# Attention projections of a fused attention and two-MoE kernel: three split products against a diagonal weight become one fp32 product per head on its own 64 rows

## Chip, core and metric

One NeuronCore of a Trainium2 chip runs the whole program. The metric is the device time of one execution in microseconds. The kernel before takes 2019.83 us, the median of three runs (2019.09 to 2023.27).

## What is computed

The reference chains three layers; the change touches the first lines of the first one.

```python
def phi(x):                                   # x: q or k, (4, 8, 576, 64)
    proj = np.einsum('bhsd,df->bhsf', x, w_phi)          # w_phi: (64, 128)
    proj = proj - np.max(np.abs(proj), axis=-1, keepdims=True)
    return np.concatenate([np.exp(proj), np.exp(-proj)], axis=-1)
q_p, k_p = (phi(q), phi(k))
kv = np.einsum('bhsf,bhsd->bhfd', k_p, v)
z = np.sum(k_p, axis=2)
num = np.einsum('bhsf,bhfd->bhsd', q_p, kv)
den = np.einsum('bhsf,bhf->bhs', q_p, z)[..., None] + 1e-06
return (num / den).astype(np.float32)
```

The result, 2304 tokens of 512 features, goes through a mixture of experts with Sinkhorn routing (8 experts, all of them applied to all tokens) and through one with a single expert per token. These two layers take most of the time.

## The kernel before

**Units and steps.** The attention stage works on eight units: a pair of batches (`bp`) times a pair of heads (`h_`). The transposed inputs hold the two heads of a pair on partitions 0 to 63 and 64 to 127, and 1152 tokens (two batches) in the free dimension, cut into nine chunks of 128 tokens. `CH` groups them into five groups per unit: four of two chunks and one of a single chunk.

**One step.** `step` is called once per group. In program order it issues `qtr` (transposes of the previous group's q projection to feature-major, L183), `proj` for one k group and for one q group of the unit before (L144), `kvm` (the k side's product with v, summed over a unit in the banks B and C, L166), `xtr` (transposes of a finished group of results, L226) and `num` (numerator and denominator of one group, L195). At a *turn*, where a unit's last k group is summed, `kvm` comes first, then `qtr`, the q projection, the k projection, `xtr` and `num`. Seven turns have a k projection in them, one per boundary between two units; the first of these has no finished result for `xtr` yet. Each engine works its instructions off in this order; the five functions write one queue per engine.

**The projection.** The weight is a 128 x 256 tile with `w_phi` twice on its diagonal, so that one product over 128 rows gives both heads. To reach fp32 accuracy with the faster fp32r format, weight and input are split into a rounded part and a rest (`wbh`, `wbl`; `hi`, `lo`), and each chunk takes three products (L151 to L153) summed in one PSUM bank. `split_in` makes the input's parts: a cast on ScalarE (L122) and a subtract on GpSimd, or on VectorE for the first unit (L123). VectorE then takes the largest magnitude per token and head straight from PSUM (L155) and subtracts it (L157), both heads at once. For k, ScalarE applies the two exponentials (L161); for q they come after the transposes (L192).

**PSUM.** Eight banks: four buffers "A" (`proj`, `xtr`), one "B" and one "C" (`kvm`), two "D" (`qtr`, `num`). When only the last unit's q groups are left (`live["tail"]`), `proj` uses C and `xtr` uses B, because the first MoE's products take A. The pool gives a new tile one of its tag's buffers, and the new tile's first writer waits for the last reader of the old one.

**After num.** `num` ends on VectorE: add, reciprocal and multiply (L219, L220, L223) read its bank and write `xn`. `xtr` transposes `xn`, ScalarE copies it to `xo` (L234) and SP writes it out.

Of the kernel before, what the change touches and what calls it, by code (L numbers as in the profile page):

```python
# [11 lines left out]
F32 = mybir.dt.float32  # L12
F32R = mybir.dt.float32r
# [3 lines left out]
ALU = mybir.AluOpType  # L17
AX = mybir.AxisListType
# [3 lines left out]
B, H, S, D = 4, 8, 576, 64  # L22
# [3 lines left out]
P = 128  # L26
# [18 lines left out]
def build(tc, a, out):  # L45
# [5 lines left out]
    live = {}  # L51
# [8 lines left out]
    V, A, G, T, SP = nc.vector, nc.scalar, nc.gpsimd, nc.tensor, nc.sync  # L60
# [3 lines left out]
    def psum(tag, shape):  # L64
        n_ps[0] += 1
        bufs = {"A": 4, "B": 1, "C": 1, "D": 2}[tag]
        return live["pp"].tile(shape, F32, tag="ps" + tag, bufs=bufs, name=f"ps{tag}{n_ps[0]}")

    def f32(ap):
        return ap.bitcast(F32)  # L70
# [25 lines left out]
    ap_ = at.enter_context(tc.tile_pool(name="at", bufs=2))  # L96
    units = [(bp, hp_) for bp in (1, 0) for hp_ in range(KD)]
    NU = len(units)
    CH = [(0, 1), (2, 3), (4, 5), (6, 7), (8,)]
# [3 lines left out]
    def load_in(u, which, g):  # L103
        bp, h_ = units[u]
        cs = slice(CH[g][0] * P, (CH[g][-1] + 1) * P)
        r = ap_.tile([P, 2 * P], F32, tag="r" + which, bufs=3, name=f"r{which}{u}{g}")
        SP.dma_start(out=r[:, 0:cs.stop - cs.start], in_=a[which + "T"][bp, h_, :, cs])
        live["r" + which, u, g] = r

    def load_v(u):  # L110
        bp, h_ = units[u]
        v = ap_.tile([P, 2, 11 * W], F32, tag="v", name=f"v{u}")
        SP.dma_start(out=v, in_=a["v"][bp, h_])
        live["v", u] = v

    def split_in(u, which, g):
        r = live.pop(("r" + which, u, g))
        n = len(CH[g]) * P
        bufs = 3 if which == "k" else 2
        hi = ap_.tile([P, 2 * P], F32R, tag="h" + which, bufs=bufs, name=f"h{which}{u}{g}")  # L120
        lo = ap_.tile([P, 2 * P], F32R, tag="l" + which, bufs=bufs, name=f"l{which}{u}{g}")
        A.copy(hi[:, :n], r[:, :n])  # L122
        (V if u == 0 else G).tensor_tensor(out=lo[:, :n], in0=r[:, :n], in1=f32(hi[:, :n]), op=ALU.subtract)  # L123
        live["s" + which, u, g] = (hi, lo)

    def warm(n):
        ps = psum("D", [P, P])
        for _ in range(n):
            T.matmul(ps, ident, ident, start=True, stop=True)

    wphi = ap_.tile([P, 2 * P], F32, bufs=1, name="wphi")
    V.memset(wphi, 0.0)
    for g in range(2):
        SP.dma_start(out=wphi[g * D:(g + 1) * D, g * P:(g + 1) * P], in_=a["w_phi"])
    for g in range(3):
        load_in(0, "k", g)
    load_v(0)
    warm(10)
    wbh = ap_.tile([P, 2 * P], F32R, bufs=1, name="wbh")
    wbl = ap_.tile([P, 2 * P], F32R, bufs=1, name="wbl")  # L140
    V.tensor_copy(wbh, wphi)
    V.tensor_tensor(out=wbl, in0=wphi, in1=f32(wbh), op=ALU.subtract)

    def proj(u, which, g):  # L144
        hi, lo = live.pop(("s" + which, u, g))
        n = len(CH[g])
        ps = psum("C" if live.get("tail") else "A", [P, 2 * n, P])
        for c in range(n):
            o = ps[:, 2 * c:2 * c + 2, :].rearrange("p h f -> p (h f)")
            cs = slice(c * P, (c + 1) * P)  # L150
            T.matmul(o, hi[:, cs], wbh, start=True, stop=False)  # L151
            T.matmul(o, hi[:, cs], wbl, start=False, stop=False)
            T.matmul(o, lo[:, cs], wbh, start=False, stop=True)  # L153
        m = ap_.tile([P, 4], F32, tag="m", bufs=4, name=f"m{which}{u}{g}")[:, 0:2 * n]
        V.tensor_reduce(out=m, in_=ps, axis=AX.X, op=ALU.max, apply_absolute_value=True)  # L155
        pr = ap_.tile([P, 4, P], F32, tag="pr" + which, name=f"pr{which}{u}{g}")[:, 0:2 * n]
        V.tensor_tensor(out=pr, in0=ps, in1=m.unsqueeze(2).to_broadcast([P, 2 * n, P]), op=ALU.subtract)  # L157
        if which == "k":
            ek = ap_.tile([P, 4, 2, P], F32, tag="eq" if u == 0 and g == 2 else "ek", bufs=2, name=f"ek{u}{g}")
            for sg in range(2):  # L160
                A.activation(out=ek[:, 0:2 * n, sg, :], in_=pr, func=AF.Exp, scale=1.0 - 2.0 * sg)  # L161
            live["ek", u, g] = ek
        else:
            live["pr", u, g] = pr
# [61 lines left out]
    def xtr(u, g):  # L226
        bp, h_ = units[u]
        xn = live.pop(("xn", u, g))
        n = len(CH[g])
        ps = psum("B" if live.get("tail") else "A", [P, n * P])  # L230
        for c in range(n):
            T.transpose(ps[:, c * P:(c + 1) * P], xn[:, 2 * c:2 * c + 2, :].rearrange("p h e -> p (h e)"), ident)
        xo = ap_.tile([P, 2 * P], F32, tag="xo", name=f"xo{u}{g}")
        A.copy(xo[:, 0:n * P], ps)  # L234
        o = bp * S2 + CH[g][0] * P
        SP.dma_start(out=xd[:, h_, o:o + n * P], in_=xo[:, 0:n * P])


    for g in range(3):
        split_in(0, "k", g)  # L240
    ones = c0.tile([P, P], F32, name="ones")
    V.memset(ones, 1.0)
    trif = wp.tile([P, 1024], F32, tag="wA11_1", name="trif")[:, 0:P]
# [36 lines left out]
    def misc_loads():  # L280
        for k in range(RB):
            SP.dma_start(out=ids[k].rearrange("(p c) o -> p (c o)", p=P), in_=sents[k == 0])
        SP.dma_start(out=x2d[NT:NT + 1, :], in_=zrow)
        SP.dma_start(out=wgf, in_=a["moe_w_gate"].rearrange("(k p) e -> p k e", p=P))
        SP.dma_start(out=emb, in_=a["moe2_expert_emb"])
        SP.dma_start(out=itau, in_=a["moe2_tau"].to_broadcast([P, 1]))
# [29 lines left out]
    def misc_trans():  # L316
        ps = psum("D", [P, KD, E])
        for k in range(KD):
            T.transpose(ps[:, k, :], emb[:, k * P:(k + 1) * P], ident[0:E, 0:E])
        V.tensor_copy(enT, ps)  # L320
# [4 lines left out]
    def load_w(kind, n):  # L325
        if n >= NGR:
            return
        e, g = divmod(n, 2)
        rs = []
        for r_ in range(2):  # L330
            t = raw() if kind == 1 or n == 0 else live["h3"].tile([P, 1024], F32, tag=f"rx{r_}", name=f"rx{n}_{r_}")
            SP.dma_start(out=t, in_=a[f"moe_w{kind}"][e, g, r_])
            rs.append(t)
        r1, r2 = rs
        rawt[kind, n] = dict(A11=r1[:, 0:512], A22=r1[:, 512:1024], A12=r2[:, 0:512], A21=r2[:, 512:1024])
# [290 lines left out]
    def bgpop(n=1):  # L626
        for _ in range(n):
            if bg:
                bg.popleft()()
# [37 lines left out]
    NG = len(CH)  # L667
# [5 lines left out]
    def at_(i):  # L673
        return order[i] if 0 <= i < len(order) else None

    for i in range((NU + 1) * NG - 1):
        p, g = i // NG, i % NG
        if i == 1:
            misc_loads()
        for which, nx in (("k", at_(i + 3)), ("q", at_(i + 3 - NG))):  # L680
            if nx:
                load_in(nx[0], which, nx[1])
        if g == 2 and p + 1 < NU:
            load_v(p + 1)
        if p >= 2:
            next(misc, None)
        if p == 4 and g == 0:
            load_w(1, 0)
        if p == 5 and g == 0:
            o_ = wops(1, 0)  # L690
            live["wsp"] = ap_

            def both(names, o_=o_):
                for nm in names.split():
                    o_[nm]()

            bg.extend(partial(both, nm) for nm in ("A11 S1r", "S3r A12", "S2r S1 A22", "S4r S3", "S2 S4"))
            bg.append(partial(load_w, 2, 0))
        if p == 5 and g == 3:
            q = []  # L700
            for t_ in ("hB11", "hB21"):
                s_ = hp.tile([P, 2, 2, TH], F32, tag=t_, name="xs" + t_)
                q += [s_[:, 0], s_[:, 1]]
            ops = x_tasks(HS[0][1], q)
            ops["load"]()
            bg.extend(ops[k_] for k_ in XFIRST)
        for which, nx in (("k", at_(i + 1)), ("q", at_(i + 2 - NG))):
            if nx and not (which == "k" and i < 2):
                split_in(nx[0], which, nx[1])
        if i == NU * NG:  # L710
            while bg:
                bgpop()
            live["tail"] = True
            o2 = wops(2, 0, {"A21": "S3"})
            bg.extend(o2[nm] for nm in ("A11", "A12", "A21", "A22"))
        step(at_(i), at_(i + 1 - NG), first if p == NU else None)
        if p == 3 and g == NG - 1:
            misc_trans()
        bgpop()
# [576 lines left out]
    tail = route_steps(0, (1, 2, 4, 6, 8, 10), (1, 2, 3, 4, 5, 6), b=8, o=9, p=11, c=12, s=13, d=14, w=15, i=(16, 16, 18, 19, 20, 21))  # L1296
# [233 lines left out]
```

## Time and profile before

| | |
|---|---|
| median of three runs | 2019.83 us (2019.09, 2019.83, 2023.27) |
| profiled execution, its own time | 2022.27 us |
| its span, first to last instruction | 2020.5 us |
| mean granted TensorE clock | 0.989 of full speed |
| attention stage, last transpose of `xn` | about 226 us after the start |
| busy over the span: PE, VectorE, ScalarE, GpSimd | 98%, 65%, 43%, 49% |

PE is TensorE's matmul queue and PEld its weight loads; DVE is VectorE, ACT ScalarE, POOL GpSimd, SP the engine that issues the transfers. A matmul's reported length contains the pipeline's end, so two rows may overlap: what a product costs is the step from its start to the next start. An fp32 product stands in the trace as two array instructions, an fp32r product or a transpose as one. The granted clock is given as a share of 2.4 GHz.

### The profile page before, as it was taken

To read this page: it belongs to the slowest core of one execution; us is meant where nothing else is said; L and a number is where in the kernel's file an instruction comes from. 1 tells how busy PE (TensorE), PEld (TensorE's weight loads), DVE (VectorE), ACT (ScalarE), POOL (GpSimd) and SP (SyncE) were. 2 spreads that over 40 slices of the span, in tenths; PEclk is the share of its full clock that TensorE was granted. 3 is DMA by queue.
4 is the path that set the end of the run, shared out by engine and by line. 5 is a ranking of instruction groups with operands and counts; after the bars stand their busy time and mean duration, and the time that the engine had idled before them with its cause. 6 is when DMAs were issued, how large, how long until landed. Compare 5 with 4: busy or idle time off the path is not lost.

```text
span 2020.5 us, 31417 instructions
## 1 busy us (share of the span) xinstructions
PE 1978.7 (98%) x11715; PEld 1901.4 (94%) x11715; DVE 1309.5 (65%) x1865; ACT 869.2 (43%) x1391; POOL 995.1 (49%) x733
## 2 busy tenths in 40 slices
PE   9999999999999999999999999999999998899998
PEld 9999999999999999999999999999999988778886
DVE  6766656466566656656665675666567444889996
ACT  5566432233333423333342333334233233777775
POOL 1255112575664747566474756647475432323332
PEclk9999999999999999999999999999999998999999
DMA  4344543543726345372644537364453344153851
GB/s 122 113 148 158 222 180 152 143 175 113 251 88 218 131 153 183 114 249 90 218 132 152 182 116 250 88 217 133 151 183 109 128 170 123 35 178 108 291 199 61
DMA packets 118979, 314.61 MB, mean 156 GB/s; under 512 B 11466, under 2 KB 65948, under 8 KB 118822
## 3 DMA queue, kind: packets, MB, share of 16 engines
q1 hardware_dynamic: 114726, 302.04, 44.8%
q0 software_dynamic: 4096, 10.51, 1.7%
q8 instruction: 95, 1.56, 0.3%
q14 instruction: 62, 0.51, 0.1%
HBM read 335.80 MB, written 32.28 MB: 182 GB/s over the span
## 4 chain that ended last, share of the span: by engine, by line
PE 76%; POOL 8%; DVE 6%; issue 5%; DMA 2%; ACT 2%; SPq 1%; POOLq 0%; DVEq 0%; ACTq 0%
PE Q L430 15%; PE Q L429 14%; PE Q L431 14%; PE psD L205 3%; PE psD L429 2%; PE psD L430 2%; PE psD L431 2%; POOL w1S L349 2%; PE psA L429 2%; PE psA L1140 2%; PE psA L431 2%; PE psA L430 2%; PE psA L1141 2%; POOL hB L477 2%; PE psA L1139 2%
## 5 line engine op out<-in xcount | busy, mean ns | idle before, releaser
L493 DVE TENSOR_TENSOR acca<-acca,Q 128x768 f32<-128x768 f32 x182 | 168.5, 949 | 133.3 <-PE Q L431 133.3
L429 PE MATMUL Q<-hT,w2S 128*128 128x384 f32 x468 | 157.5, 336 | 4.1 <-DVE rd L489 4.1
L477 POOL TENSOR_TENSOR hB<-rb,hB 128x768 fp32r<-128x768 f32 x39 | 72.1, 1848 | 180.4 <-ACT hB L474 180.4
L429 PE MATMUL Q<-xT,w1S 128*128 128x384 f32 x468 | 156.4, 334 | 0.9 <-ACT ra L498 0.9
L430 PE MATMUL Q<-hT,w2S 128*128 128x384 f32 x468 | 156.4, 334 | 0.0
L431 PE MATMUL Q<-hT,w2S 128*128 128x384 f32 x468 | 156.4, 334 | 0.0
L431 PE MATMUL Q<-xT,w1S 128*128 128x384 f32 x468 | 156.3, 334 | 0.0
L430 PE MATMUL Q<-xT,w1S 128*128 128x384 f32 x468 | 156.3, 334 | 0.0
L349 POOL TENSOR_TENSOR w1A<-raw,w1A 128x512 fp32r<-128x512 f32 x48 | 62.1, 1294 | 159.4 <-ACT w1A L348 86.2
L493 DVE TENSOR_TENSOR accb<-accb,Q 128x768 f32<-128x768 f32 x91 | 84.3, 949 | 68.0 <-PE Q L431 68.0
L1113 DVE TENSOR_TENSOR s1l<-rw,s1h 128x1024 fp32r<-128x1024 f32 x88 | 112.4, 1332 | 9.6 <-ACT s1h L1112 7.4
L489 DVE TENSOR_TENSOR Q<-Q,ra 128x768 f32<-128x768 f32 x39 | 37.7, 967 | 124.6 <-PE Q L431 124.6
L498 ACT COPY ra<-Q 128x768 f32<-128x768 f32 x39 | 31.3, 802 | 176.0 <-PE Q L431 156.3
L429 PE MATMUL Q<-xB,w1A 128*128 128x384 f32 x312 | 104.3, 334 | 0.7 <-DVE accb L851 0.7
L431 PE MATMUL Q<-hB,w2A 128*128 128x384 f32 x312 | 104.3, 334 | 0.0
L431 PE MATMUL Q<-xB,w1A 128*128 128x384 f32 x312 | 104.2, 334 | 0.0
L430 PE MATMUL Q<-xB,w1A 128*128 128x384 f32 x312 | 104.2, 334 | 0.0
L429 PE MATMUL Q<-hB,w2A 128*128 128x384 f32 x312 | 104.2, 334 | 0.0
L430 PE MATMUL Q<-hB,w2A 128*128 128x384 f32 x312 | 104.2, 334 | 0.0
L477 POOL TENSOR_TENSOR hT<-ra,hT 128x768 fp32r<-128x768 f32 x39 | 72.0, 1845 | 64.2 <-ACT hT L474 64.2
L477 POOL TENSOR_TENSOR hT<-rd,hT 128x768 fp32r<-128x768 f32 x39 | 72.3, 1854 | 57.0 <-ACT hT L474 57.0
L1079 POOL DMA_INDIRECT xgs<-x2d,idt x22 | 35.6, 1619 | 126.3 <-DVE gt L1077 126.0
(431 smaller groups left out, 6702.9 us busy)
## 6 DMA issues: line engine op xcount, KB each, us to landing
xT<-xpd SPq DMA_DIRECT2D x120, 768.0 KB
rw<-in_moe_w SPq DMA_DIRECT2D x176, 512.0 KB
xB<-xpd SPq DMA_DIRECT2D x90, 768.0 KB
raw<-in_moe_w SPq DMA_DIRECT2D x34, 512.0 KB
gate<-gd SPq DMA_DIRECT2D x45, 384.0 KB
rx<-in_moe_w SPq DMA_DIRECT2D x30, 512.0 KB
xpd<-xT SPq DMA_DIRECT2D x12, 768.0 KB
xpd<-xB SPq DMA_DIRECT2D x9, 768.0 KB
```

Source lines behind the costliest of these rows:

```text
L205: T.matmul(ps[:, off:off + w], eq[:, sg, h_, ci * P:(ci + 1) * P], kvz[:, h_, sg, o:o + w], start=(sg == 0), stop=(sg == 1))
L349: eng.tensor_tensor(out=t[:, 1], in0=r(nm), in1=f32(t[:, 0]), op=ALU.subtract)
L429: T.matmul(bank, w[:, 0, j, k, :], x[:, 0, k, :], start=start and k == 0, stop=False, skip_group_check=True)
L430: T.matmul(bank, w[:, 0, j, k, :], x[:, 1, k, :], start=False, stop=False, skip_group_check=True)
L431: T.matmul(bank, w[:, 1, j, k, :], x[:, 0, k, :], start=False, stop=stop and k == 1, skip_group_check=True)
L477: eng.tensor_tensor(out=hb[nm][:, 1], in0=src, in1=f32(hb[nm][:, 0]), op=ALU.subtract)
L489: V.tensor_tensor(out=out, in0=x, in1=y, op=op)
L493: V.tensor_tensor(out=z, in0=z, in1=ps, op=op)
L1113: V.tensor_tensor(out=lo, in0=r, in1=f32(hi), op=ALU.subtract)
L1139: T.matmul(ps[hf], th[:, k, :], wh[:, cs], start=(k == 0), stop=False)
L1140: T.matmul(ps[hf], tl[:, k, :], wh[:, cs], start=False, stop=False)
L1141: T.matmul(ps[hf], th[:, k, :], wl[:, cs], start=False, stop=(k == KD - 1))
```

## The change

`proj` takes the raw fp32 input. Per chunk and head it issues one fp32 product whose operands lie on that head's 64 partitions, against a plain copy of `w_phi` on the same 64 partitions. Each head has a PSUM tile of its own: two of A per projection, in the tail one of C and one of B. Reduce and subtract are issued per head, half the size each. The weight tile is 128 x 128, with two transfers as before; its zeroing and its split are gone. `split_in` and its calls are gone. The raw tiles get four buffers instead of three. `xtr` takes its bank from D at all times.

```diff
     def load_in(u, which, g):
...
-        r = ap_.tile([P, 2 * P], F32, tag="r" + which, bufs=3, name=f"r{which}{u}{g}")
+        r = ap_.tile([P, 2 * P], F32, tag="r" + which, bufs=4, name=f"r{which}{u}{g}")
...
-    def split_in(u, which, g):
-        r = live.pop(("r" + which, u, g))
-        n = len(CH[g]) * P
-        bufs = 3 if which == "k" else 2
-        hi = ap_.tile([P, 2 * P], F32R, tag="h" + which, bufs=bufs, name=f"h{which}{u}{g}")
-        lo = ap_.tile([P, 2 * P], F32R, tag="l" + which, bufs=bufs, name=f"l{which}{u}{g}")
-        A.copy(hi[:, :n], r[:, :n])
-        (V if u == 0 else G).tensor_tensor(out=lo[:, :n], in0=r[:, :n], in1=f32(hi[:, :n]), op=ALU.subtract)
-        live["s" + which, u, g] = (hi, lo)
...
-    wphi = ap_.tile([P, 2 * P], F32, bufs=1, name="wphi")
-    V.memset(wphi, 0.0)
+    wphi = ap_.tile([P, P], F32, bufs=1, name="wphi")
     for g in range(2):
-        SP.dma_start(out=wphi[g * D:(g + 1) * D, g * P:(g + 1) * P], in_=a["w_phi"])
+        SP.dma_start(out=wphi[g * D:(g + 1) * D, :], in_=a["w_phi"])
...
-    wbh = ap_.tile([P, 2 * P], F32R, bufs=1, name="wbh")
-    wbl = ap_.tile([P, 2 * P], F32R, bufs=1, name="wbl")
-    V.tensor_copy(wbh, wphi)
-    V.tensor_tensor(out=wbl, in0=wphi, in1=f32(wbh), op=ALU.subtract)

     def proj(u, which, g):
-        hi, lo = live.pop(("s" + which, u, g))
+        r = live.pop(("r" + which, u, g))
         n = len(CH[g])
-        ps = psum("C" if live.get("tail") else "A", [P, 2 * n, P])
+        ps = [psum(t_, [P, n, P]) for t_ in ("CB" if live.get("tail") else "AA")]
         for c in range(n):
-            o = ps[:, 2 * c:2 * c + 2, :].rearrange("p h f -> p (h f)")
-            cs = slice(c * P, (c + 1) * P)
-            T.matmul(o, hi[:, cs], wbh, start=True, stop=False)
-            T.matmul(o, hi[:, cs], wbl, start=False, stop=False)
-            T.matmul(o, lo[:, cs], wbh, start=False, stop=True)
+            for h_ in range(2):
+                hs = slice(h_ * D, h_ * D + D)
+                T.matmul(ps[h_][:, c, :], r[hs, c * P:(c + 1) * P], wphi[hs, :], start=True, stop=True)
         m = ap_.tile([P, 4], F32, tag="m", bufs=4, name=f"m{which}{u}{g}")[:, 0:2 * n]
-        V.tensor_reduce(out=m, in_=ps, axis=AX.X, op=ALU.max, apply_absolute_value=True)
         pr = ap_.tile([P, 4, P], F32, tag="pr" + which, name=f"pr{which}{u}{g}")[:, 0:2 * n]
-        V.tensor_tensor(out=pr, in0=ps, in1=m.unsqueeze(2).to_broadcast([P, 2 * n, P]), op=ALU.subtract)
+        for h_ in range(2):
+            mh = m.rearrange("p (c h) -> p h c", h=2)[:, h_]
+            V.tensor_reduce(out=mh, in_=ps[h_], axis=AX.X, op=ALU.max, apply_absolute_value=True)
+            V.tensor_tensor(out=pr.rearrange("p (c h) f -> p h c f", h=2)[:, h_], in0=ps[h_], in1=mh.unsqueeze(2).to_broadcast([P, n, P]), op=ALU.subtract)
...
     def xtr(u, g):
...
-        ps = psum("B" if live.get("tail") else "A", [P, n * P])
+        ps = psum("D", [P, n * P])
```

**TensorE's queue at a turn, before.** `psA` and `psD` are PSUM tiles, `hq`/`lq` and `hk`/`lk` the split inputs, `prq` a q projection, `xn` a finished result, `eq` and `kvz` the operands of `num`; in brackets the engines' counters that an instruction waits for.

```order
L190 MATMUL psD_1075<-ident,prq_1028 128x128 x3
L151 MATMUL psA_1082<-wbh,hq_998 128x256
L152 MATMUL psA_1082<-wbl,hq_998 128x256
L153 MATMUL psA_1082<-wbh,lq_999 128x256 [waits Pool_49]
...
L232 MATMUL psA_1107<-ident,xn_1050 128x128 [waits DVE_49,Activation_49]
L205 MATMUL psD_1112<-kvz_1071,eq_1074 128x65 [waits Activation_49] x2
L205 MATMUL psD_1112<-kvz_1071,eq_1074 128x65 x6
L190 MATMUL psD_1139<-ident,prq_1091 128x128 [waits DVE_49,PE_49]
```

The same place with the change:

```order
L175 MATMUL psD_981<-ident,prq_939 128x128 x2
L136 MATMUL psA_988<-wphi,rq_842 128x128 [waits DMAHW0_49]
L136 MATMUL psA_989<-wphi,rq_842 128x128
L136 MATMUL psA_988<-wphi,rq_842 128x128
L136 MATMUL psA_989<-wphi,rq_842 128x128
L136 MATMUL psA_1000<-wphi,rk_766 128x128 [waits DMAHW3_49]
...
L217 MATMUL psD_1015<-ident,xn_964 128x128 [waits DVE_49,PE_49]
L190 MATMUL psD_1020<-kvz_977,eq_980 128x65 [waits PE_49,Activation_49]
L190 MATMUL psD_1020<-kvz_977,eq_980 128x65 x7
L175 MATMUL psD_1039<-ident,prq_995 128x128 [waits DVE_49,PE_49]
```

The order of the steps is the same. The projections alternate between two banks and wait for their transfer instead of GpSimd; `xtr` (now L217) writes a `psD` tile between `qtr` (now L175) and `num` (now L190). The addresses in the built program put the last `qtr` shown, `psD_1039`, into the bank of `psD_1020`, the tile of the `num` just ahead of it, and so at the six turns that have an `xtr` and a k projection; before, `psD_1139` had the bank of `psD_1075`, the `qtr` one step earlier.

**VectorE's queue at that turn with the change**, from the first read of the q projection to the next step; `mq`, `mk` are the maxima, `d` the denominators.

```order
L141 TENSOR_REDUCE mq_994<-psA_988 128x2 [waits PE_49]
L142 TENSOR_TENSOR prq_995<-psA_988,mq_994 128x2x128 [waits DVE_49]
L141 TENSOR_REDUCE mq_994<-psA_989 128x2 [waits PE_49]
L142 TENSOR_TENSOR prq_995<-psA_989,mq_994 128x2x128 [waits DVE_49]
L141 TENSOR_REDUCE mk_1006<-psA_1000 128x2 [waits PE_49]
L142 TENSOR_TENSOR prk_1007<-psA_1000,mk_1006 128x2x128 [waits DVE_49,Activation_49]
L141 TENSOR_REDUCE mk_1006<-psA_1001 128x2 [waits PE_49]
L142 TENSOR_TENSOR prk_1007<-psA_1001,mk_1006 128x2x128 [waits DVE_49]
L204 TENSOR_SCALAR d_1029<-psD_1020 128x4 [waits PE_49]
L205 RECIPROCAL d_1029<-d_1029 128x4 [waits DVE_49]
L208 TENSOR_TENSOR xn_1030<-psD_1020,d_1029 128x256 [waits DVE_49]
```

Eight operations on projections stand ahead of the three that read `psD_1020`; before there were four, each twice as wide.

## Rows read from the trace of the kernel before

**Rows 1.** The page, busy time, share of the span and instructions.

```profile
PE 1978.7 (98%) x11715; PEld 1901.4 (94%) x11715; DVE 1309.5 (65%) x1865; ACT 869.2 (43%) x1391; POOL 995.1 (49%) x733
```

**Rows 2.** Stretches: us, busy (x count) per engine, PEclk, DMA share, GB/s; attention.

```profile
60.00:80.00 20.00, 20.00 (x182) 20.00 (x182) 15.38 (x38) 12.10 (x31) 5.97 (x9) 1.00 0.28 90
```

**Rows 3.** Groups by line, 0 to 240 us, PE: count | busy us, mean ns | idle.

```profile
L176 PE MATMUL psB<-v,ek 128*128 128x65 f32 (+1 forms) x288 | 56.4, 278 | 0.0
...
L151 PE MATMUL psA<-wbh,hk 128*128 128x256 f32 x72 | 23.2, 322 | 0.0
...
L151 PE MATMUL psA<-wbh,hq 128*128 128x256 f32 x65 | 18.9, 291 | 0.0
```

**Rows 4.** Groups by line, same stretch, the splits on GpSimd and ScalarE.

```profile
L123 POOL TENSOR_TENSOR lk<-rk,hk 128x256 fp32r<-128x256 f32 (+1 forms) x35 | 23.8, 679 | 91.1 <-ACT hk L122 73.1 <-PE psD L205 11.2 <-PE psA L153 5.3
...
L122 ACT CAST hk<-rk 128x256 fp32r<-128x256 f32 (+1 forms) x40 | 15.4, 385 | 3.2 <-DMA rk<-in_kT 3.0
```

**Rows 5.** Timeline, PE, the turn at 71.6 us: start us, length us, engine, instruction.

```profile
71.65 0.39 PE L176 MATMUL psC<-v,ek 128*128 128x65 f32 x2
...
71.88 0.39 PE L176 MATMUL psB<-v,ek 128*128 128x65 f32 x2
...
72.91 0.36 PE L151 MATMUL psA<-wbh,hq 128*128 128x256 f32 x1
...
73.11 0.28 PE L152 MATMUL psA<-wbl,hq 128*128 128x256 f32 x1
...
74.31 0.28 PE L153 MATMUL psA<-wbh,lk 128*128 128x256 f32 x1
...
74.54 1.90 PE L205 MATMUL psD<-kvz,eq 128*128 128x65 f32 x16
...
76.27 0.61 PE L190 MATMUL psD<-ident,prq 128*128 128x128 f32 x4
```

**Rows 6.** Timeline, VectorE, the same turn.

```profile
73.91 0.69 DVE L155 TENSOR_REDUCE mq<-psA 128x4 f32<-128x512 f32 x1 [0.41 <-PE psA L153]
74.63 0.69 DVE L157 TENSOR_TENSOR prq<-psA,mq 128x512 f32<-128x512 f32 x1
...
76.63 0.15 DVE L219 TENSOR_SCALAR d<-psD 128x4 f32<-128x4 f32 x1
...
77.03 0.42 DVE L223 TENSOR_TENSOR xn<-psD,d 128x256 f32<-128x256 f32 x1
```

**Rows 7.** Timeline, VectorE, a single-chunk group at 43 us.

```profile
43.45 0.41 DVE L155 TENSOR_REDUCE mk<-psA 128x2 f32<-128x256 f32 x1
...
43.97 0.42 DVE L157 TENSOR_TENSOR prk<-psA,mk 128x256 f32<-128x256 f32 x1
```

**Rows 8.** Timeline, PE, three-row products among full ones at 1806 us.

```profile
1805.48 0.39 PE L1140 MATMUL psA<-s1h,xtl 128*128 128x512 f32 x1
1805.71 0.39 PE L1141 MATMUL psA<-s1l,xth 128*128 128x512 f32 x1
1806.03 0.63 PE L1073 MATMUL psB<-ones,idr 3*128 3x1 f32 x4
1806.58 0.66 PE L1121 MATMUL psA<-ident,xgs 128*128 128x128 f32 x4
```

**Rows 9.** Stretches after idle spells of PE; the column 1.00 or 0.50 is PEclk.

```profile
11.70:15.10 3.40, 3.40 (x19) 3.40 (x18) 1.95 (x5) 1.64 (x4) 0.00 (x0) 0.50 0.83 173
...
331.00:335.00 4.00, 2.76 (x17) 2.44 (x16) 3.61 (x12) 0.41 (x2) 0.00 (x0) 1.00 0.99 363
...
1663.80:1667.10 3.30, 3.30 (x13) 2.99 (x12) 0.29 (x1) 0.89 (x2) 2.31 (x2) 0.50 0.02 5
```

**Rows 10.** Timeline, PE, the idle spells before them, in brackets with the releaser.

```profile
10.49 0.46 PE L176 MATMUL psC<-v,ek 128*128 128x130 f32 x2 [2.57 <-DMA v<-in_v]
...
333.13 0.39 PE L797 MATMUL psC<-cs,ones 128*128 128x8 f32 x2 [1.24 <-DVE cs L794]
...
1661.90 0.18 PE L931 MATMUL psB<-oh,tri 128*128 128x48 bf16 x1 [1.33 <-DVE oh L921]
```

More of the change, by code (lines that the diff above doesn't have):

```diff
@@ L236, in xtr @@
         SP.dma_start(out=xd[:, h_, o:o + n * P], in_=xo[:, 0:n * P])
-    for g in range(3):
-        split_in(0, "k", g)
     ones = c0.tile([P, P], F32, name="ones")
@@ L706, in build @@
             bg.extend(ops[k_] for k_ in XFIRST)
-        for which, nx in (("k", at_(i + 1)), ("q", at_(i + 2 - NG))):
-            if nx and not (which == "k" and i < 2):
-                split_in(nx[0], which, nx[1])
         if i == NU * NG:
```

## The prediction

> **What bounds the kernel now.** I read the busy table first: TensorE's matmul queue is busy for 98% of the span [rows 1]. An average over stages says nothing about the stage that changes, so the second view is the table of stretches. In the attention stage, about 10 to 226 us, PE shows 20.00 busy of 20 us, VectorE 15.38, ScalarE 12.10 and GpSimd 5.97 [rows 2]. PE is the bound there, with no slack, and VectorE is the next engine. Third, the groups by line give the counts: each of the three products of a projection stands 72 times for k and 72 for q, 65 of these in the banks A and seven in the tail's [rows 3]. Fourth, the timeline of one hand-over between two head pairs (a "turn") shows how far the other engines lag behind PE [rows 5, 6].
>
> **The change part by part.** Times are against the profiled execution, 2022.27 us for a span of 2020.5. The three timed runs have the median 2019.83, 2.4 us lower; I carry the difference over to that median.
>
> *Removed on PE.* From L152 at 73.11 to L153 at 74.31 lie ten projection products in 1.20 us, 0.12 each [rows 5]. 432 of them: 51.8 us, all on the path.
>
> *Added on PE.* 288 fp32 products on 64 rows. One fp32 product is two array instructions here: L176 is written 144 times per bank and stands 288 times [rows 3], and two take 71.88 - 71.65 = 0.23 us, 0.112 to 0.115 each [rows 5]. The reported length is 0.275, so the next weights load and the next product already run beside the last one; what is paid is the step. 576 steps of 0.112 are 64.5 us if they follow one another: 13 more than what goes. That is the upper bound. The lower bound is two at a time: two head halves use different rows of the array and different banks, so never more than two run together. They can pair only from the second instruction on, so each of the 42 groups keeps one unpaired step: 64.5 / 2 + 42 x 0.112 = 37.0 us, a gain of 14.8. No row of before has two row positions in turn; the nearest row, the three-row products of L1073, shows four at one position, and four at one position must queue for the same cells. It does not bear on different positions, so I take the lower bound and keep the upper one as a rival. The Trainium skill (TensorE: Matmul & The Clock Gate, Part 3, measured speedup) gives 3.07 and not 4 for four row tiles; as an estimate from that page two halves would gain 1.54, 42 us, and the sum below would be 5 us higher. No row here shows it.
>
> *The array changes its shape.* Products on fewer rows stand among full ones already [rows 8]. A full product there steps 1805.71 - 1805.48 = 0.23. From the last full one to the next lie 1806.58 - 1805.71 = 0.87 us, so 0.64 beyond its own step, for four small instructions. They step 0.112, as above, to 0.127 (0.63 less the last one's reported 0.25, over three), and leave 0.13 to 0.19 for going in and coming out; I take 0.17, since the way in alone shows 0.32 - 0.23 = 0.09. The built program enters the 64-row form 42 times (k and q of a step lie next to each other): 42 x 0.17 = 7.1 us. Hidden behind neighbours it would be 0; 8 is the other end.
>
> *VectorE.* One reduce and one subtract of 512 elements become two of 256 each. Half-size rows last 0.41 and 0.42 [rows 7] against 0.69 and 0.69 for the full size [rows 6]: about 0.3 us more per group, 64 full groups, and 0.15 for each of the 16 single-chunk groups: 22 us in all, 2.2 per 20 us of stage. 15.38 + 2.2 stays under 20, so as throughput it costs nothing. As latency it does not (next term).
>
> *ScalarE and GpSimd.* 80 casts of 0.385 and 70 subtracts of 0.68 go [rows 4], and ten subtracts on VectorE. PE had no idle time behind them in this stage, so they give nothing back; the cover is PE's own work.
>
> *A new wait on PE.* `xtr` moves from the four buffers A to the two buffers D, which then take three tiles per step (`qtr`, `xtr`, `num`) instead of two. The built program puts, at six turns (the first has no result yet, the last no k), the next `qtr` into the bank that `num` just filled: the order shows it waiting for DVE right behind `num`. So PE must wait until VectorE has read `num`, and VectorE comes to that only behind both projections. From the turn at 72.91 [rows 5, 6]: VectorE starts 1.00 us after the first product, begins `num`'s reads at 76.63 and ends them at 77.03 + 0.42 = 77.45, while PE began the next `qtr` at 76.27. With today's durations that wait would be 1.2 us. With the change VectorE starts earlier (half a tile: about 0.5 us after the first product), needs eight steps of 0.45 instead of 2.7, then the 0.82 of `num`: 0.5 + 3.6 + 0.8 = 4.9. PE is there after 1.0 (16 steps, paired) + 0.1 + 0.1 + 1.73 (`num`) = 2.95. The stall is 1.9 us, six times: 11.4 us. Behind the waiting `qtr` stand the step's projections, `kvm` and `num`, so all of PE shifts. Late next is `eq` on ScalarE, which has slack. The Trainium skill (TensorEngine Tiling (Array Packing), PSUM Bottleneck) states the general rule: tiling speeds up TensorE but not the emptying of PSUM. Without the emptying of the banks the sum so far would be -7.7 us, with it it is +3.7, so the trace bears the rule out for the turns and, by the 15.38 of 20 us, not for the stage.
>
> *DMA and queues.* Loads, their number and place on SP stay; the two weight loads carry the same 32 KB. A raw tile is now held until PE has read it, and has a fourth buffer for that. At a step of about 5 us, and loads issued two steps ahead, I cost it at nothing; if a load took 10 us, PE would wait for it.
>
> *The clock.* An idle PE can lose its clock. After 2.57 us idle [rows 10] the granted clock is 0.50 for 3.4 us [rows 9], the 1.2 GHz level; after 1.24 us it stays at 1.00; 1.33 us, with little work behind it, is followed by 0.50 again. Stalls of 1.9 us lie between. One fall costs half of 3.4, so 1.7 us; six would cost 10. I take three: 5.1 us, with 0 and 10 as ends.
>
> **Sum:** -51.8 + 37.0 + 7.1 + 11.4 + 5.1 = **+9 us**, 2031 on the profiled run's scale, **2029** on the median's.
>
> **The rivals.**
> *One after another.* The halves queue for the weights path. For: fp32 products of 65 columns step at 0.112 although they stream half of what a new one does, so the load is what they wait for [rows 5], and L1073's three rows are no faster [rows 8]. Against: no row shows two positions. Then +12.7 (64.5 - 51.8) + 7.1, and the stalls shrink, because PE arrives later (1.8 + 0.2 + 1.73 = 3.7 against VectorE's 4.9): 6 x 1.2 = 7.2. Sum +27: 2047. This is also the case in which the change does not do what its separate banks are laid out for.
> *Faster: the stall is covered.* Halves run together, and VectorE reaches `num` in time. The gain without stalls and falls is 7.7, so it stays faster by over 4 us (0.2%, about what a measurement of this kernel can tell from no change) only if a turn costs under 0.6 us. Price: down to 2012. For: VectorE idles 4.6 of 20 us [rows 2]. Against: from its first reduce to the end of `num`'s reads the turn leaves it next to nothing free, four operations of 0.69 and 0.82 of `num`'s in 3.54 us [rows 6].
> *Cancelling.* Halves together, shape changes partly hidden, stalls of 1.3 and no fall of the clock: -14.8 + 4 + 7.8 = -3, and 0 with the shape changes in full: 2017 to 2020.
>
> **How the numbers follow.** My case, halves together with the stall, 0.53 (its own range 2021 to 2035: from shape changes at 5 us and no fall to 8 us and six falls); one after another 0.27; cancelling 0.12; covered 0.08. Faster is 0.08, same 0.12, slower 0.80. The range for 8 in 10 leaves out the covered case, part of the cancelling one and what lies above the serial sum, whose stalls and falls can add a few us: 2020 to 2050.
>
> **What would show it.** Step between projection instructions: near 0.056 on average right, 0.112 means the first rival. At each turn an idle row before the `qtr` line released by DVE, 1.9 us, six times; none there refutes the forecast and gives the faster case. Before and after each projection group about 0.1 us. The granted clock under 1.00 in stretches behind turns tells the last term. Wrong outright would be stage ends before 226 us, or a wait on loads of q or k.

## The result, and the profile after

The changed kernel takes **2037.66 us** (median; 2035.91 to 2039.51) against 2019.93: 1.0085 times the time before, 95% interval 1.0067 to 1.0102, 17.7 us slower. The forecast had the sign, its mechanism and the range right, and about half of the size (2029). The profiled execution took 2039.51 us, its span is 2037.7. Single runs of one kernel differ, and their mean granted clock with them: of ten runs of `xfirst` below seven took 2016.3 to 2018.4 us at 0.991 to 0.994 and three 2027.7 to 2030.2 at 0.985 or 0.986, of nine runs of `warm` three took 2039.2 to 2041.2 at 0.986 or 0.987; the ratios take all runs in, the medians do not show the long ones.

The page's first part, after:

```profile
PE 1985.9 (97%) x11859; PEld 1895.4 (93%) x11859; DVE 1321.9 (65%) x2012; ACT 848.7 (42%) x1311; POOL 950.0 (47%) x663
```

PE still looks full, as in [rows 1], so the average again says nothing of the stage. The place where the stage ends does: the last `xtr` starts at 242.06 us and not at 225.80. **16.3 of the 17.2 us of span are lost in the attention stage.** Two views tell where. First PE's waits from 40 to 200 us (line waited for: us in all, times, longest):

```profile
PE psD L175 <- DVE xn L208: 9.9, 6, 1.7
PE psD L175 <- ACT xo L219: 0.3, 1, 0.3
```

L175 is `qtr`: six waits of 1.65 us, one at each of six turns, released by VectorE's last read of `num` (L208). That is the forecast's wait, at its line, as often as forecast. Second, the table of stretches (us, then busy us per engine, granted clock, DMA share, GB/s): the stretch of [rows 2], the one in which the kernel before had its clock fall [rows 9], and four in which the changed kernel has one.

```profile
60.00:80.00 20.00, 19.73 (x180) 18.14 (x180) 14.65 (x48) 8.60 (x19) 0.58 (x1) 0.92 0.33 99
```

```profile
11.70:15.10 3.40, 3.40 (x37) 3.13 (x36) 1.89 (x5) 1.44 (x4) 0.00 (x0) 1.00 0.90 244
49.41:63.06 13.65, 13.11 (x74) 12.18 (x74) 6.09 (x21) 4.75 (x10) 0.00 (x0) 0.50 0.33 97
83.54:86.95 3.41, 3.41 (x24) 2.98 (x22) 1.45 (x4) 1.18 (x3) 0.00 (x0) 0.50 0.22 60
138.16:141.57 3.41, 3.32 (x21) 2.80 (x22) 0.94 (x3) 2.20 (x5) 2.22 (x2) 0.50 0.22 60
192.77:196.18 3.41, 3.34 (x21) 2.82 (x22) 0.96 (x3) 2.34 (x5) 1.81 (x1) 0.50 0.12 40
```

GpSimd's 5.97 us of splits are gone (0.58), as is part of ScalarE's work, and nothing got faster by that. PE stands at 0.50, the 1.2 GHz level, for 13.65 + 3 x 3.41 = 23.9 us, each time from within a turn's wait or from at most 0.5 us behind its end (the first wait is over at 49.95, the second at 83.12). Half of such a stretch is lost: 12.0 us, or 11.6 without the 0.7 us of them that lie inside the waits.

One turn of the changed kernel, PE's timeline (start us, length us, then the instruction; in brackets the idle time before it and its releaser), to be held against [rows 5]:

```profile
106.75 0.71 PE L136 MATMUL psA<-wphi,rq 64*128 64x128 f32 x8
107.29 0.61 PE L136 MATMUL psA<-wphi,rk 64*128 64x128 f32 x8
107.84 0.33 PE L217 MATMUL psD<-ident,xn 128*128 128x128 f32 x1
108.05 2.00 PE L190 MATMUL psD<-kvz,eq 128*128 128x65 f32 x16
111.70 0.63 PE L175 MATMUL psD<-ident,prq 128*128 128x128 f32 x4 [1.65 <-DVE xn L208]
```

The 1.65 us count from the reported end of `num`'s last product. From start to start, which is what is paid, `qtr` comes 1.93 us behind that product (it starts at 108.05 + 2.00 - 0.28 = 109.77) instead of the 0.11 of steps without a wait: a turn loses 1.82 us, the six together 10.9.

Eight array instructions in 107.29 - 106.75 = 0.54 us: singly at 0.112 they would need 0.90. In the trace they start in pairs, the second some 7 ns behind the first. **The halves do run together.** VectorE in the same turn, against [rows 6]:

```profile
107.49 0.42 DVE L141 TENSOR_REDUCE mq<-psA 128x2 f32<-128x256 f32 x1 [1.68 <-PE psA L136]
...
110.39 0.42 DVE L142 TENSOR_TENSOR prk<-psA,mk 128x256 f32<-128x256 f32 x1
110.73 0.15 DVE L204 TENSOR_SCALAR d<-psD 128x4 f32<-128x4 f32 x1
...
111.13 0.42 DVE L208 TENSOR_TENSOR xn<-psD,d 128x256 f32<-128x256 f32 x1
```

Eight steps from 107.49 to 110.73, without a gap, then `num`'s reads to 111.55; PE starts `qtr` 0.15 later. And ScalarE, which has to free the other of the two banks, the one that `xtr` filled:

```profile
110.91 1.15 ACT L146 ACTIVATE ek<-prk 128x512 f32<-128x512 f32 x2 [2.91 <-DVE d L204]
111.97 0.25 ACT L219 COPY xo<-psD 128x128 f32<-128x128 f32 x1
```

The copy of `xtr`'s bank stands behind the exponentials of k's projection, and ends at 112.22, later still. So at a turn both banks D are held by work queued behind both projections; it is not that the wrong one was picked.

### The profile page after: what moved, and what is told of

It reads as the page before. It is cut to its first block, busy times and chain, and to the rows that moved or that the text cites. A ratio compares the mean times of both kernels' runs of the same rounds, so it can differ in the third digit from the quotient of the medians.

```text
span 2037.7 us, 31647 instructions
## 1 busy us (share of the span) xinstructions
PE 1985.9 (97%) x11859; PEld 1895.4 (93%) x11859; DVE 1321.9 (65%) x2012; ACT 848.7 (42%) x1311; POOL 950.0 (47%) x663
## 4 chain that ended last, share of the span: by engine, by line
PE 76%; POOL 9%; DVE 6%; issue 5%; ACT 2%; DMA 2%; SPq 1%; POOLq 0%; DVEq 0%; ACTq 0%
PE Q L413 14%; PE Q L414 14%; PE Q L412 14%; PE psD L190 3%; PE psD L412 2%; POOL w1S L332 2%; PE psD L413 2%; PE psD L414 2%; PE psA L136 2%; POOL hB L460 2%; PE psC L161 2%; PE psA L1120 2%; PE psA L1121 2%; PE psA L1119 2%; PE psA L412 2%
## 5 line engine op out<-in xcount | busy, mean ns | idle before, releaser
L412 PEld LDWEIGHTS Q<-hT,w2S 128*128 128x128 f32 x468 | 87.8, 188 | 8.0 <-issue 8.0
```

Source lines behind the costliest of these rows:

```text
L412: T.matmul(bank, w[:, 0, j, k, :], x[:, 0, k, :], start=start and k == 0, stop=False, skip_group_check=True)
```

## The experiments

Theory: the loss is six waits and the clock falls that idle time brings; the products themselves got cheaper. Each run is given with its median, its ratio to runs of the kernel before on the same chip, and the start of the last `xtr` in its profile ("attention ends").

**1. Last `xtr` ahead of the projections at a turn** (`xfirst`).

```diff
         for t in qq:
             qtr(*t)
+        if turn:
+            while xq:
+                xtr(*xq.pop(0))
```

> At a turn the last xtr is issued right behind qtr, ahead of the two projections, so that its copy on ScalarE and then num's reads no longer decide the bank of the next qtr; no instruction is added or removed. Theory (the loss is the six stalls and the clock that falls behind them): the six waits of qtr go, 9.9 us, and with them the half clock of 40 to 226 us (23.9 us at 0.50 in the changed kernel, 12 us of time). Attention ends near 242.06 - 9.9 - 12 = 220 to 223 instead of 242.06, and the time is 2015 to 2019, at or a little under the kernel before. Rival one (the clock falls because 64-row products keep half the array idle, not because PE stands still): the waits go, the half clock stays, attention ends near 232, time 2028. Rival two (the wait only moves to another line): over 6 us of waits stay in the turns, attention ends after 236.

Measured: 2016.85 us, ratio 0.9998 (0.998 to 1.0017); attention ends at 221.51, 20.6 us sooner than in the changed kernel. PE's waits from 10 to 243 us, and the stretch as a whole:

```profile
PE psD L412 <- ACT accb L832: 0.7, 1, 0.7
PE psC L136 <- ACT kvz L165: 0.7, 1, 0.7
PE psC L161 <- DMA v<-in_v: 0.7, 1, 0.7
PE psD L175 <- ACT xo L219: 0.3, 1, 0.3
```

```profile
10.00:243.00 233.00, 231.07 (x2108) 216.12 (x2107) 166.00 (x515) 118.45 (x255) 39.25 (x27) 1.00 0.46 147
```

No wait at a turn is left on the list and the clock is 1.00. Same instructions, 20.6 us: 10.9 of waits (start to start) and 11.6 of clock, less some 2 us of smaller delays. One of these stands behind each turn, where the next two projections take 100.73 - 99.47 = 1.26 us instead of 1.09. Both rivals fall: 64-row products alone do not bring the clock down, and the wait did not move. ScalarE's timeline at a turn shows why:

```profile
95.97 1.08 ACT L177 ACTIVATE eq<-psD 128x512 f32<-128x512 f32 x2
96.94 0.27 ACT L219 COPY xo<-psD 128x128 f32<-128x128 f32 x1
```

The copy now comes right behind `eq` and ends at 97.21, long before PE wants the bank (the next `qtr` at 98.94).

**2. The wait filled with spare products** (`warm`).

```diff
             dx.append(t)
+        if turn and qq and k:
+            t = qq[-1]
+            pw = psum("C", [P, W])
+            for j_ in range(7):
+                T.matmul(pw, ident, live["kvz", t[0]][:, 0, 0, 0:W], start=True, stop=True)
```

> Seven spare fp32 products of 65 columns (0.23 us each, 1.6 us together) are put behind num at each turn, into a bank that nothing reads; they fill the stall and change no wait. Theory (idle time brings the clock down): the turns stay as long as they were, idle time there falls from 1.65 to under 0.3 us, and the half clock of 40 to 226 us goes nearly whole: attention ends near 242 - 12 = 230, to 232 if the spare products overrun the stall, time 2025 to 2028. Rival one (64-row products bring it down): half clock as before, attention ends at 242 or later, time 2037 or more.

Measured: 2028.29 us, ratio 1.0053 (1.0031 to 1.0075); attention ends at 232.34. The whole stretch, then PE at one turn:

```profile
10.00:243.00 233.00, 231.40 (x2148) 216.53 (x2146) 159.31 (x505) 112.95 (x244) 39.24 (x27) 1.00 0.42 135
```

```profile
76.16 1.73 PE L653 MATMUL psC<-kvz,ident 128*128 128x65 f32 x14
77.97 0.63 PE L175 MATMUL psD<-ident,prq 128*128 128x128 f32 x4
```

At the six turns with a wait the spare products take the idle time and leave the turn as long as it was: `qtr` starts 1.93 us behind `num`'s last product (76.04), as in the changed kernel. The clock stays at 1.00. Only the first turn, which has no wait, gets longer, by 1.6 us. Attention ends 9.7 us sooner: 11.6 of clock less these 1.6, and 0.3 of smaller steps. This separates the two halves of the loss, and ties the falls to idle time, as far as the profile goes: of the three long runs no trace is kept. The median lies 0.3 us over the bound of 2028; the profiled run took less.

**3. All chunks of head 0 first, then head 1** (`headmajor`).

```diff
-        for c in range(n):
-            for h_ in range(2):
+        for h_ in range(2):
+            for c in range(n):
```

> Within a projection all chunks of head 0 stand first, then those of head 1, instead of head by head in turn; the same products, the same banks. Theory (two halves run together only when neighbours in the queue use different rows, and starts keep the queue's order): a two-chunk projection of 8 array instructions goes from 4 pairs to about 7 single steps, so 3 x 0.11 = 0.33 us more, over 64 of them 21 us, less some 3 us of shorter stalls because the bank of head 0 is full earlier: attention ends near 255 to 262, time 2050 to 2057. Rival (the array looks ahead in its queue and pairs anyway, or the order does not matter): step and time as in the changed kernel, 2036 to 2039.

Measured: 2037.47 us, ratio 1.009 (1.0073 to 1.0107), the changed kernel's time; the six waits are 9.9 us again, and attention ends at 240.74. My theory of this run fell: the pairs stay, as the rival had it. PE's timeline at a turn:

```profile
102.84 0.72 PE L136 MATMUL psA<-wphi,rq 64*128 64x128 f32 x8
103.39 0.71 PE L136 MATMUL psA<-wphi,rk 64*128 64x128 f32 x8
104.03 0.33 PE L217 MATMUL psD<-ident,xn 128*128 128x128 f32 x1
```

Eight instructions again start within 103.39 - 102.84 = 0.55 us, in pairs, although four of one row position stand together in the program. The instruction that signals VectorE that head 0's bank is full, the fourth of eight in the program, is the seventh to start, and VectorE's first reduce begins 0.74 us behind the first product in both orders (103.58 here, 107.49 above). See the last section.

The rival's "step as in the changed kernel" does not hold to the end. The two projections take 104.03 - 102.84 = 1.19 us up to the next line, against 107.84 - 106.75 = 1.09; over the stage the projections take 2.8 us more. That attention does not end later is the clock's doing: this profile has 17.1 us at half clock and not 23.9.

**4. `xtr` back in the banks A** (`xtr_in_a`).

```diff
-        ps = psum("D", [P, n * P])
+        ps = psum("A", [P, n * P])
```

> Undoes the move of xtr alone: its transposes go to the four buffers A again, which now carry five tiles per step (two heads of k, two of q, xtr). Theory (what is late is VectorE's and ScalarE's work behind k's projection, whichever bank has to wait for it): the wait of qtr goes, xtr waits for the subtract of q's first head instead, by the rows of the turn at 107 us 108.37 - 107.84 = 0.5 us, and the next projection for the banks of k; half or more of the 9.9 us stays in the turns, attention ends at 230 to 240. Rival (the two buffers D are the whole trouble): no waits over 0.3 us in the turns, attention ends near 220, time 2017.

Measured: 2027.01 us, ratio 1.0039 (1.0022 to 1.0055). Waits from 10 to 243 us:

```profile
PE psA L217 <- DVE prq L142: 3.7, 6, 0.6
PE psA L136 <- ACT xo L219: 2.4, 6, 0.4
PE psA L217 <- DVE hB L422: 1.8, 1, 1.8
...
```

At the turns, undoing the move leaves 6.1 of the 9.9 us, cut into waits of 0.6 and 0.4: four banks are one too few for five tiles a step. No turn loses its clock. In the profiled run attention still ends at 240.67, and 20.5 us right behind the start run at half clock, after three waits of 0.4 to 0.5 us close together; without them it would be 230. The last `xtr` itself waits 1.8 us for the first MoE (the third row): this edit gives `xtr` a bank of A in the tail too, where the kernel before took B, so there it is not the move undone. Its other runs go down to 2024.66 at a clock of 0.993.

**5. VectorE's operations at full size again** (`merge`): both heads' banks as one tile of two neighbouring banks.

```diff
...
+            pw = live["pa"].tile([P, 2, 512], F32, tag="psA", bufs=2, name=f"psA{n_ps[0]}")
+            ps = [pw[:, h_, 0:n * P].rearrange("p (c f) -> p c f", f=P) for h_ in range(2)]
...
+            V.tensor_reduce(out=mv, in_=pv, axis=AX.X, op=ALU.max, apply_absolute_value=True)
+            V.tensor_tensor(out=pr.rearrange("p (c h) f -> p h c f", h=2), in0=pv, in1=mv.unsqueeze(3).to_broadcast([P, 2, n, P]), op=ALU.subtract)
```

> The half-size VectorE operations alone undone (one tile of two banks per projection), the order at the turn as in the changed kernel. Theory (the stall is VectorE's latency behind both projections: eight steps of 0.45 us against four of 0.7): num's reads end 0.5 to 0.9 us earlier, the wait of qtr shrinks from 1.65 to 0.8 to 1.2 us, 5 to 7 us over six turns, and with waits as short as the 1.24 us of the kernel before, after which the clock stayed, the half clock goes mostly too: attention ends at 226 to 232, time 2021 to 2028. Rival one (the wait is set by the banks, not by VectorE's pace): 1.65 us as before, time 2036 or more. Rival two (any wait of a microsecond brings the clock down): the waits shrink and the half clock stays at 14 us or more, attention ends at 234 to 240.

Measured: 2028.48 us, ratio 1.0036 (1.0024 to 1.0048); attention ends at 233.74. The waits, and the four stretches at half clock:

```profile
PE psD L194 <- DVE xn L227: 6.9, 6, 1.2
...
```

```profile
75.30:78.70 3.40, 3.35 (x22) 2.83 (x23) 0.96 (x2) 1.58 (x4) 0.00 (x0) 0.52 0.21 58
129.70:133.10 3.40, 3.40 (x24) 2.90 (x23) 1.69 (x3) 1.89 (x5) 2.61 (x3) 0.51 0.20 58
157.40:160.80 3.40, 3.40 (x25) 2.85 (x23) 1.51 (x3) 1.19 (x4) 2.01 (x2) 0.55 0.46 120
184.30:187.70 3.40, 3.13 (x21) 2.61 (x21) 0.86 (x3) 2.53 (x6) 1.81 (x1) 0.51 0.29 96
```

The half-size operations were worth 0.5 us of each wait (1.65 to 1.15), as the theory had it. But four falls of 3.4 us stay: rival two is nearer on the clock, and the stage ends 1.7 us behind the range of the theory. Waits of 1.15 us suffice for a fall, so the 1.24 us in [rows 10] that cost nothing is no safe mark.

**6. Both halves on rows 0 to 63** (`samerows`), on top of the diff of run 1.

```diff
-                hs = slice(h_ * D, h_ * D + D)
+                hs = slice(0, D)
```

> As the run with xtr first, but the products of head 1 read rows 0 to 63 too, with the weight there: head 1 gets head 0's projections, so what is computed is not the reference. Same number of instructions and the same banks, one row position instead of two. Theory (the halves pair because they stand on different rows): array instructions of projections step 0.112 us singly, 576 of them instead of 288 pairs, attention ends 22 to 27 us later than with xtr first, 244 to 249 us, time 2039 to 2046. Rival (separate banks or small products are enough to pair): pairs stay, time 2014 to 2019.

Measured: 2047.67 us, ratio 1.0153 (1.0121 to 1.0185); attention ends at 248.30, at clock 1.00. One projection with the line behind it:

```profile
118.39 1.05 PE L136 MATMUL psA<-wphi,rq 64*128 64x128 f32 x8
119.37 0.43 PE L161 MATMUL psC<-v,ek 128*128 128x65 f32 x2
```

0.98 us for what took 0.54: single steps of 0.112. Two row positions, and not the separate banks, make the pairs, and they are worth 26.8 us here. The first rival of the prediction would have been this, and it was priced well (27.5 us between the two sums of steps). The median is 1.7 us above the expected range, the stage inside it.

**7. One fp32 product on all 128 rows, diagonal weight, no splits** (`diag_xfirst`), on top of the diff of run 1.

```diff
...
-                T.matmul(ps[h_][:, c, :], r[hs, c * P:(c + 1) * P], wphi[hs, :], start=True, stop=True)
...
+            T.matmul(o, r[:, c * P:(c + 1) * P], wphi, start=True, stop=True)
...
```

> One fp32 product per chunk on all 128 rows, 256 columns, with the diagonal weight of the kernel before but without splits; VectorE's operations in full size, xtr first at the turns. No 64-row form, no change of the array's shape. Theory (an fp32 instruction of 130 columns steps 0.108 us, so its columns set the step, and 256 columns need 0.213): 288 array instructions of 0.213 us are 61 us against some 49.6 us for the halves with their shape changes; attention ends 9 to 13 us later than with xtr first, 230 to 235 us, time 2025 to 2031. Rival (the step is set per instruction, whatever its columns): 288 x 0.112 = 32 us, attention ends near 204, time near 2000, and the 64-row form is the wrong way to drop the splits.

Measured: 2026.57 us, ratio 1.0026 (1.0015 to 1.0037); attention ends at 230.87, 9.4 us later than with the halves. Timeline:

```profile
120.84 1.03 PE L136 MATMUL psA<-wphi,rq 128*128 128x256 f32 x4
121.71 0.33 PE L159 MATMUL psC<-v,ek 128*128 128x65 f32 x2
```

Four instructions of 256 columns take 0.87 us, 0.217 each, where 65 and 130 columns both take 0.112: at this width columns set the step. The 64-row form is the better way to drop the splits, shape changes and all. Run 1 has VectorE's operations in half size; against run 10, which has them in full size like this run, the halves end the stage 11.9 us sooner.

**8. The kernel before with `xtr` in D alone** (`before_xtr_in_d`).

```diff
-        ps = psum("B" if live.get("tail") else "A", [P, n * P])
+        ps = psum("D", [P, n * P])
```

> The kernel before with one part of the change alone: xtr's transposes go to the two buffers D. Splits, diagonal weight and full-size VectorE operations stay. Theory (the waits at the turns come from the move of xtr, behind both projections on VectorE, and idle time brings the clock down whatever products surround it): six waits of 1.2 to 1.3 us, as worked out ahead for the durations of before, 7 to 8 us together, and falls of the clock behind several of them as in the run with one two-bank tile (14 us at half clock there): attention ends at 236 to 242 instead of 225.80, time 2030 to 2037. Rival one (the clock falls only where 64-row products surround the wait): waits as above, no half clock beyond the one of before, attention ends near 233, time 2027. Rival two (without the faster products TensorE never reaches the bank too early): no waits, time 2019 to 2023.

Measured: 2031.87 us, ratio 1.0052 (1.0035 to 1.0069); attention ends at 237.18. Waits, and the stretches at half clock:

```profile
PE psD L190 <- DVE xn L223: 6.2, 5, 1.5
PE psC L176 <- ACT ek L161: 2.4, 2, 1.3
PE psD L190 <- ACT xo L234: 1.3, 2, 1.0
...
```

```profile
133.30:136.70 3.40, 3.40 (x19) 3.40 (x18) 1.37 (x3) 2.37 (x7) 2.55 (x3) 0.52 0.17 43
188.30:191.70 3.40, 3.40 (x19) 3.40 (x18) 1.21 (x2) 2.58 (x6) 2.44 (x2) 0.54 0.08 24
```

This one line alone costs 0.5%: at the six turns 7.2 us of waits of `qtr` (the 6.2, and the 1.0 of the third row), near the six of 1.2 that the forecast had worked out for the durations of before, and two falls, with no 64-row product in the program. Fewer falls than I expected (6.8 us at half clock, not 14).

**9. The kernel before with the order of run 1 alone** (`before_xfirst`): the diff of run 1.

> The kernel before with the order of the cure alone: xtr ahead of the projections at the turns. Theory (the gain of the cured versions over before is that of the products; before has no wait at its turns to cure): attention ends within 1 us of 225.80, time within 0.2% of before. Rival (part of the cured versions' lead is the order itself): 3 us or more faster.

Measured: 2020.69 us, ratio 0.9997 (0.9988 to 1.0007); attention ends at 225.58. The order gives the kernel before nothing.

**10. Order and two-bank tile together** (`merge_xfirst`): the diffs of runs 1 and 5.

> The turn order of the run with xtr first, and both heads' banks as one tile of two neighbouring banks, so that VectorE again does one reduce and one subtract of 512 elements per projection. Theory (TensorE bounds the stage, and with the turns cured VectorE's 22 us of extra work is covered): VectorE's busy time falls by about 20 us, attention still ends at 219 to 222 us, and the time stays within 3 us of the run with xtr first, 2014 to 2019. Rival (the half-size operations still delay TensorE in many small waits): attention ends before 217, time 2012 or less.

Measured: **2014.88 us, ratio 0.9968 (0.9956 to 0.998)**, faster than both kernels; attention ends at 218.94. PE's waits from 40 to 219 us, whole:

```profile
PE psC L150 <- ACT kvz L184: 0.7, 1, 0.7
```

VectorE is busy for 1304.1 us against 1319.7 in run 1 (15.6 less, 20 expected), and that gives 2.6 us in the stage, inside the 3 expected: most of VectorE's extra work was covered once the turns were cured.

## Why the prediction was right in sign and short in size

Its own terms, for the attention stage (+16.3 us):

| term | forecast | measured |
|---|---|---|
| products, paired, against the three of before, with shape changes | -51.8 + 37.0 + 7.1 = -7.7 | -3.8 |
| six waits, from start to start | 11.4 | 10.9 |
| clock | 5.1 | 9.9 |
| first `kvm`, which waits for v, starts at 9.82 and not 10.49 | none | -0.7 |
| sum | +9 | +16.3 |

*Removed.* 0.12 a step held: full groups of twelve take 1.39 us from first to last start.

*Halves together.* Held as a mechanism, and runs 6 and 3 show that the row position makes it. The likeliest case was this one. A pair steps 0.112, but the first of a group 0.213: the 42 unpaired steps that I allowed (0.112 each) are there in size. The Trainium skill (TensorE: Matmul & The Clock Gate, Part 3, measured speedup) had led to an estimate of 1.54 for two halves. From first to last start eight instructions take 0.883 us in run 6 and 0.444 here, 1.99; my estimate was too low for this form.

*Shape changes: mis-sized.* I took 0.17 from one place in [rows 8], with 7.1 us in all and 8 as an end. Between start and start, a full group of k and q (16 instructions) has 0.203 on the way in, 0.89 inside, 0.202 on the way out: 1.295 us against 0.028 + 1.394 + 0.121 = 1.543 before. Over 41 groups (21 of that size, 15 with 12 instructions, 1.181 to 1.072; five smaller) that is -6.9. But the line behind pays too. Both kernels without a wait, one step each; first before, then run 1:

```profile
76.27 0.61 PE L190 MATMUL psD<-ident,prq 128*128 128x128 f32 x4
76.63 0.36 PE L151 MATMUL psA<-wbh,hk 128*128 128x256 f32 x1
...
78.15 0.39 PE L176 MATMUL psC<-v,ek 128*128 128x130 f32 x2
...
79.88 0.39 PE L232 MATMUL psA<-ident,xn 128*128 128x128 f32 x2
```

```profile
104.53 0.61 PE L175 MATMUL psD<-ident,prq 128*128 128x128 f32 x4
105.06 0.71 PE L136 MATMUL psA<-wphi,rk 64*128 64x128 f32 x8
...
106.16 0.44 PE L161 MATMUL psC<-v,ek 128*128 128x65 f32 x2
...
107.99 0.39 PE L217 MATMUL psD<-ident,xn 128*128 128x128 f32 x2
```

Projections 1.52 to 1.10; but `qtr` ahead 0.36 to 0.53 (the way in, counted above), and `kvm` behind 1.73 to 1.83. `kvm`'s extra 0.10 (medians from first to last start 1.622 and 1.724) comes 30 times: 3.1 us. In run 7, which never takes the 64-row form, it is not there (1.620). So the 0.17 for going in and coming out was right (0.09 each, over a step of 0.112); what I had at nothing is the 0.10 behind it. A round trip costs about 0.28, and the sum of the products is -6.9 + 3.1 = -3.8.

*VectorE.* As throughput nothing: held to within the 2.6 us of run 10. As latency it set the wait; forecast 4.9 us from the first product to the end of `num`'s reads, measured 111.55 - 106.75 = 4.8.

*The wait.* Six times at the line named. The idle row is 1.65 us, but the forecast's 1.9 counted starts, and so counted a turn loses 1.82. PE's next start would have been 109.77 + 0.11 = 109.88, 3.1 us behind the first product and not 2.95, in part the shape changes again.

*ScalarE, GpSimd, DMA.* Nothing, as forecast: no PE wait from 40 to 200 us is on a load of q or k.

*The clock: the step that failed.* "I take three", each 3.4 us long. There were four, and one lasted 13.65 us; together they take 11.6 us and not 5.1. The table's 9.9 subtracts 1.7 because the fall of before at 11.7 us [rows 9] did not happen in this profile; run 9 has none there either, with the same start, so that is no merit of the change. The upper end of 10 for six falls was too low by the same cause: their length was taken from the two that the trace of before had.

*The range and the rivals.* 2037.66 lies in 2020 to 2050, a little above my case's own range (2021 to 2035), which the clock passed. "Faster, the stall is covered" ended at 2012 in my working; run 1 is that case made, 2016.85.

**Open.** Which wait loses the clock: in the profiled runs waits of 1.65 us did so at four turns of six (changed kernel; run 3 too, but not the same four), 1.15 us at four of six (run 5), 1.0 to 1.5 us at two of six (run 8), 0.6 us at none (run 4), and a filled wait never (run 2). Why one fall lasted four times as long, and one of run 3 twice, was not tried. Whether the longer runs of runs 1 and 2 lost their clock at the start, as the profiled run 4 did, is a guess: their traces are not there.

## What to carry to other kernels

When a change moves one more tile into a small set of banks, walk each bank's release through the engine that empties it, in that engine's own order: here a transpose behind two projections had its copy, and `num` its reads, queued behind work that PE did not need yet, and moving one transpose ahead of them was worth 20 us. Price a PE stall with the clock it may lose, not by its own length alone: here stalls of 10.9 us took 11.6 us more with them. Cheaper products save only what their neighbours do not pay, so measure the line ahead and the line behind as well.

## What the runs showed that was not expected

*The array runs ahead in its queue across row positions.* In run 3 products of both positions start 13 ns apart, although four array instructions of the first position stand ahead of the other's first in the program; the signalling instruction, fourth of eight in the program, starts seventh, 0.44 us behind the first. The Trainium skill (TensorE: Matmul & The Clock Gate, Part 3) says that products start and end in program order, strictly first in, first out. For products at different row positions these starts do not agree with it; the ends in a trace are modelled, so of those no run here tells. Writing the halves in turn was not needed for the pairs; it saved 0.10 us in most steps, 2.8 us in the stage.

*Leaving the 64-row form is paid twice.* 0.202 us instead of some 0.11 to the first full product, and 0.10 more inside the next 16 (1.724 us from first to last start, against 1.620 in run 7 without the 64-row form). The Trainium skill (TensorEngine Tiling (Array Packing), Key Properties) states that a change of tiling mode drains TensorE. The rows agree, and put about 0.28 us on a round trip.
